# Attention values of three batches as float32 products of two heads side by side, in a fused attention and two-layer-MoE kernel

## The chip, the cores and the metric

One core of a Trainium2 chip runs the whole kernel. The metric is the device time in microseconds: before the change 1043.67 us, the median of 3 runs (1043.12 to 1044.32).

## The reference

Three stages follow each other. The change is in the last line of the first.

```python
# q, k, v: (4 batches, 8 heads, 576, 64) float32; f: (4, 8, 576)
scores = scale * q @ k^T;  cum = cumsum(log(clip(f)))
scores = where(causal, -1e9, scores + cum[..., :, None] - cum[..., None, :])
attn = exp(scores - max);  attn = attn / (sum(attn) + 1e-09)
x = attn @ v                               # then (4*576 tokens, 8*64)
x = leaky_relu(x @ w_in) @ w_out           # 512 -> 2048 -> 512
out = ((x @ w_a) * (x @ w_b)) @ w_o2       # 512 -> 1536 -> 512
```

## The kernel before

**Two kinds of product.** TensorE (PE) multiplies either operands typed float32r, of which a number is carried as a high and a low part (xh and xl, gh and gl, ph and pl), so that a product takes two or three matmuls, or plain float32 operands, where one matmul of the program makes two records of the trace. `evac` (L455 to L457) makes the two parts of a PSUM tile: ACT copies the high part, DVE subtracts it from the source for the low part. `split` does the same from SBUF (L138, L139).

**Attention in blocks.** A batch of 576 queries is done in two blocks: block 0 has the first 256 queries, block 1 the next 256 and, for two heads at once, the last 64 of each (tile p4: 64 partitions for the even head, 64 for the odd). `att_scores` makes scores, decay, maximum, exponential and the normalized probabilities of one head, with the queries on partitions. `att_values` turns (transposes) the probabilities in tiles of 128 by 128 on PE (`pp`), so that keys are on partitions, and multiplies them with v. Heads 2hp and 2hp+1 are a pair.

**The values, batch 0.** Probabilities and v are plain float32. For both heads, u = 0 and 1, the matmul's 64 value columns go to their own half of the output's partitions; the two heads' matmuls alternate, and a dependency added by hand holds the first until the second head's probabilities are there:

```python
av[u * 64 : u * 64 + 64, i0 * P : 256], vhl[:, kt, u, :], phs[u][:, a0 : a0 + 2 - i0, :],   # L533
```

**The values, batches 1 to 3.** v is split into parts side by side (`vhl`, 64 high and 64 low columns), the turned probabilities into `ph` and `pl`. Each head has its own product, two matmuls for a tile of 128 keys:

```python
for n, part in enumerate((slots, pl.rearrange("p a b c -> p (a b) c"))):
    pe_att.matmul(
        av[:, i0 * P : 256], vhl[:, kt, j, :, :], part[:, a0 : a0 + 2 - i0, :], ...   # L545 to L548
```

ACT and DVE then add the two halves of `av` (L553, L554), and after the second head the pair's 256 columns are split into the MoE's input tiles xh and xl. `att_last` turns p4 of the pair in five tiles, splits them, makes ten matmuls (`av4`, turned probabilities as weights, all four v parts moving), and ACT and DVE scale and add into x4 (L607, L608). After block 1's last pair `att_tail` turns x4 on PE (`ppx`) and splits it.

**What sets the order.** The first block is written out by hand (`FIRST`). After it the blocks are generators: the scores of one head run `beside` the values of the head before, and the last queries of a pair are chained behind its second head's values (`att_steps`). The blocks of batches 1 to 3 are interleaved with the first MoE's units (`l1` at L902 writes `h`, `l2` at L932 writes `y`; three matmuls of 256 columns a product). [...] Tiles are named buffers: `ph`, `pl`, `vs`, `vhl`, `xn` have one each, PSUM tag `ps` three.

Of the kernel before, what the change touches and what calls it, by code (L numbers as in the profile page):

```python
# [26 lines left out]
def kernel(  # L27
# [105 lines left out]
    def f32(ap):  # L133
        return ap.bitcast(F32)
# [126 lines left out]
    x4, p4s, stats, qks, xns, vhls, phs, cums, lasts, lastk = ({} for _ in range(10))  # L261
# [197 lines left out]

    def att_values(b, r, h, st):  # L460

        hp, j = h // 2, h % 2
        nk = 2 * P if r == 0 else S
        tok0 = b * S + (0 if r == 0 else 2 * P)
        nm = f"{b}_{r}_{h}"
        pair = (b, r, hp)
        ps = st["ps"]
        if j == 0:
            full, rest = nk // P, nk % P
            if b == 0:  # L470
                vs = ap_.tile([P, 5, 2, 64], F32, tag=("vs", "vhl")[hp % 2], name=f"vn_{nm}")
            else:
                vs = ap_.tile([P, 5, 2, 64], F32, tag="vs", name=f"vs_{nm}")
            for u in range(2):
                nc.sync.dma_start(vs[:, :full, u, :], v[b, h + u, : full * P, :].rearrange("(c p) d -> p c d", p=P))
                if rest:
                    nc.sync.dma_start(vs[:rest, full, u, :], v[b, h + u, full * P : nk, :])
            if b == 0:
                vhls[pair] = vs
                if rest:  # L480
                    nc.gpsimd.memset(vs[rest:, full, :, :], 0.0)
            else:

                vhl = vhls[pair] = ap_.tile([P, 5, 2, 2, 64], F32R, tag="vhl", name=f"vhl_{nm}")
                if rest:
                    nc.gpsimd.memset(f32(vhl[rest:, full, :, :, :]), 0.0)
                for x, c in ((P, slice(0, full)), (rest, slice(full, full + 1))):
                    if x:
                        split(vhl[:x, c, :, 0, :], vhl[:x, c, :, 1, :], vs[:x, c, :, :], nc.vector)
        vhl = vhls[pair]  # L490
        yield
        if b == 0:
            ph = phs[j] = ap_.tile([P, 4, 2, P], F32, tag=("ph", "pl")[j], name=f"ph_{nm}")
        else:
            ph = ap_.tile([P, 4, 2, P], F32R, tag="ph", name=f"ph_{nm}")
            pl = ap_.tile([P, 4, 2, P], F32R, tag="pl", name=f"pl_{nm}")
        slots = ph.rearrange("p a b c -> p (a b) c")
        if r == 0:

            at = {(0, 0): 1, (0, 1): 2, (1, 1): 0}  # L500
            parts = [(((1, 1), (0, 0), (0, 1)), slots[:, 0:3, :])]
        else:
            at = {(kt, i): 2 * kt + i for kt in range(4) for i in range(2)}
            parts = [([(kt, i) for kt in range(3 + i)], ph[:, : 3 + i, i, :]) for i in range(2)]
        for z, (tiles, hi) in enumerate(parts):
            pp = ps_a.tile([P, 4, P], F32, tag="ps", bufs=3, name=f"pp_{nm}_{z}")
            for m, (kt, i) in enumerate(tiles):
                pe_att.transpose(pp[:, m, :], ps[i][:, kt * P : kt * P + P], ident)
            if b == 0:
                st["second"] = act_att.copy(hi, pp[:, : len(tiles), :])  # L510
            else:
                lo = pl[:, : 3 + z, z, :] if r else pl.rearrange("p a b c -> p (a b) c")[:, 0:3, :]
                evac(hi, lo, pp[:, : len(tiles), :])
            yield
        if r == 0:
            yield
        if b == 0:
            phs[j] = slots
        if b == 0:
            if j == 0:  # L520
                return

            av = ps_a.tile([P, T1], F32, tag="ps", bufs=3, name=f"av_{nm}")
            nkt = 2 * r + 2
            for kt in range(nkt):
                i0 = 1 if kt == nkt - 1 else 0
                a0 = at[kt, i0]
                for u in range(2):
                    made = pe_att.matmul(
                        av[u * 64 : u * 64 + 64, i0 * P : 256], vhl[:, kt, u, :], phs[u][:, a0 : a0 + 2 - i0, :],  # L530
                        start=(kt == 0), stop=(kt == nkt - 1),
                    )
                    if kt == u == 0:  # L533
                        tc.add_manual_dep(made.ins, st["second"].ins.name, SYNC, reason="both heads at once")
            ch, cl = x_chunk(tok0 // T1)
            evac(ch[:, hp, :], cl[:, hp, :], av)
            yield
            return
        av = ps_a.tile([P, 256], F32, tag="ps", bufs=3, name=f"av_{nm}")
        nkt = 2 * r + 2  # L540
        for kt in range(nkt):
            i0 = 1 if kt == nkt - 1 else 0
            a0 = at[kt, i0]
            for n, part in enumerate((slots, pl.rearrange("p a b c -> p (a b) c"))):
                pe_att.matmul(  # L545
                    av[:, i0 * P : 256], vhl[:, kt, j, :, :], part[:, a0 : a0 + 2 - i0, :],
                    start=(kt == 0 and n == 0), stop=(kt == nkt - 1 and n == 1),
                )  # L548
        if j == 0:
            xns[pair] = ap_.tile([P, 256], F32, tag="xn", bufs=1, name=f"xn_{nm}")  # L550
        xt = xns[pair]
        a, o = j * 64, 64 - j * 64
        act_att.copy(xt[a : a + 64, :], av[o : o + 64, :])  # L553
        dve_att.tensor_tensor(out=xt[a : a + 64, :], in0=av[a : a + 64, :], in1=xt[a : a + 64, :], op=ALU.add)  # L554
        yield
        if j == 0:
            return
        p0 = 0
        while p0 < 256:
            c = (tok0 + p0) // T1  # L560
            c0 = tok0 + p0 - c * T1
            n = min(256 - p0, T1 - c0)
            ch, cl = x_chunk(c)
            split(ch[:, hp, c0 : c0 + n], cl[:, hp, c0 : c0 + n], xt[:, p0 : p0 + n], nc.vector)
            p0 += n
        yield

    def att_last(b, hp, rec4):
# [5 lines left out]
        ph = ap_.tile([P, 5, P], F32 if b == 0 else F32R, tag="ph", name=f"ph4_{nm}")  # L574
        nc.gpsimd.memset(f32(ph[64:, 4, :]) if b else ph[64:, 4, :], 0.0)
        if b:
            pl = ap_.tile([P, 5, P], F32R, tag="pl", name=f"pl4_{nm}")
            nc.gpsimd.memset(f32(pl[64:, 4, :]), 0.0)
        for k0, k1, w in ((0, 4, P), (4, 5, S - 4 * P)):
            pp = ps_a.tile([P, 4, P], F32, tag="ps", bufs=3, name=f"pp{k1}_{nm}")  # L580
            for kt in range(k0, k1):
                pe_att.transpose(pp[:w, kt - k0, :], p4[:, kt * P : kt * P + w], ident)
            if b == 0:
                act_att.copy(ph[:w, k0:k1, :], pp[:w, : k1 - k0, :])
            else:
                evac(ph[:w, k0:k1, :], pl[:w, k0:k1, :], pp[:w, : k1 - k0, :])
            yield
        if hp == 0:
            x4[b] = ap_.tile([P, HP // 2, P], F32, tag="x4", name=f"x4_{b}")
        if b == 0:  # L590
            av4 = ps_a.tile([P, 2, 64], F32, tag="ps", bufs=3, name=f"av4_{nm}")
            for kt in range(5):
                pe_att.matmul(av4, ph[:, kt, :], vhl[:, kt, :, :], start=(kt == 0), stop=(kt == 4))
            for u in range(2):
                rows_ = slice(u * 64, u * 64 + 64)
                act_att.mul(x4[b][64 * (hp % 2) : 64 * (hp % 2) + 64, hp // 2, rows_], av4[rows_, u, :], rec4[rows_, :])
            yield
            return
        av4 = ps_a.tile([P, 2, 2, 64], F32, tag="ps", bufs=3, name=f"av4_{nm}")
        for kt in range(5):  # L600
            pe_att.matmul(av4, ph[:, kt, :], vhl[:, kt, :, :, :], start=(kt == 0), stop=False)
            pe_att.matmul(av4, pl[:, kt, :], vhl[:, kt, :, :, :], start=False, stop=(kt == 4))
        xa = p4[:, 0:64]
        for u in range(2):
            rows_ = slice(u * 64, u * 64 + 64)
            rec = rec4[rows_, :]
            act_att.mul(xa[rows_, :], av4[rows_, u, 0, :], rec)  # L607
            dve_att.scalar_tensor_tensor(  # L608
                out=x4[b][64 * (hp % 2) : 64 * (hp % 2) + 64, hp // 2, rows_], in0=av4[rows_, u, 1, :], scalar=rec, in1=xa[rows_, :], op0=ALU.mult, op1=ALU.add
            )  # L610
# [48 lines left out]
    def first_block():  # L659
# [189 lines left out]
        def h(p, j):  # L849
            ph = ap_.tile([P, 4, 2, P], F32, tag=("ph", "pl")[j], name=f"ph_f{p}_{j}")  # L850
            x = got["ph", p, j] = ph.rearrange("p a b c -> p (a b) c")
# [410 lines left out]
    def att_steps(n):  # L1262
# [21 lines left out]
        for h in range(H):  # L1284
# [3 lines left out]
            if h % 2 == 1 and blocks[n][1] == 1:  # L1288
                second = chain(second, att_last(blocks[n][0], h // 2, st["rec4"]))
# [64 lines left out]
    for i in range(2, NB1 - 2):  # L1354
        for pr in range(NF1 // 2):
            work(i, pr)
            if pr == 0:
                for _ in att_steps(i + 1):
                    pass
                if i % 2 == 0:  # L1360
                    att_tail(i // 2)
# [139 lines left out]
```

## Time and profile before

| | |
|---|---|
| median of 3 runs | 1043.67 us (1043.12 to 1044.32) |
| the profiled execution, its span | 1049.02 us, 1047.2 us |
| PE busy, share of the span | 1017.6 us, 97% |
| PE weight loads | 942.7 us, 90% |
| DVE, ACT, POOL busy | 758.1, 586.2, 181.6 us |
| attention of batches 1 to 3 on PE | about 150 to 531 us |
| mean granted TensorE clock | 0.988 |

Matmuls are pipelined: a record of one lasts longer than the time until the next one starts. What a matmul costs PE is therefore read from the starts that follow each other, not from its length. A float32r matmul and a float32 one both carry "f32" in their shapes; the names of the operands tell them apart (float32: `vn`, `vs_f`, `kn`, `ident`; float32r: `vhl`, `ks`, `homer`). A row "x16" merges records of one kind that follow each other, at the shape of the first.

### The profile page before, as it was taken

What the parts mean: (1) busy time and instruction counts of PE and PEld (TensorE: products, weight loads), DVE (VectorE), ACT (ScalarE), POOL (GpSimd) and SP (SyncE); (2) the same over time, 40 slices, a digit from 0 to 9 for tenths busy, and PEclk for the clock granted to TensorE, in tenths of its full rate; (3) what the DMA queues carried; (4) which work ended last, traced back from release to release, by engine and by line L of the source; (5) the groups of instructions that cost most, each with busy time, mean ns of one, the idle gap of its engine ahead of it and who ended that gap; (6) DMA issues with size and microseconds to landing.
All of it is one profiled execution on the core that took longest, in us unless ns stands there. A gap on an engine that the chain in (4) does not pass through costs nothing.

```text
span 1047.2 us, 20390 instructions
## 1 busy us (share of the span) xinstructions
PE 1017.6 (97%) x7383; PEld 942.7 (90%) x7383; DVE 758.1 (72%) x1593; ACT 586.2 (56%) x1222; POOL 181.6 (17%) x414
## 2 busy tenths in 40 slices
PE   7789999999999999999999999999999999899998
PEld 6667879999999999999999998888888888799998
DVE  5869757877777777767657656787687775988872
ACT  6758777887787778868645454231323221364430
POOL 3505423334133332424100000000000000000000
PEclk9989999999999999999999999999999999999999
DMA  8788234433452334513067423222351334667721
GB/s 217 217 260 252 46 72 103 92 78 70 82 128 51 94 58 88 130 19 80 6 242 255 129 77 113 81 91 93 118 160 41 131 116 131 198 180 200 198 66 41
DMA packets 230499, 125.80 MB, mean 120 GB/s; under 512 B 144704, under 2 KB 212160, under 8 KB 230400
## 3 DMA queue, kind: packets, MB, share of 16 engines
q1 hardware_dynamic: 224784, 118.67, 41.2%
q10 hardware_dynamic: 5616, 5.84, 1.6%
q8 instruction: 58, 0.95, 0.4%
q14 instruction: 41, 0.34, 0.1%
HBM read 95.29 MB, written 29.17 MB: 119 GB/s over the span
## 4 chain that ended last, share of the span: by engine, by line
PE 81%; DMA 5%; ACT 3%; DVE 3%; issue 1%; SPq 1%; POOL 0%; ACTq 0%; DVEq 0%; POOLq 0%
PE y L932 15%; PE h L902 15%; PE o L1237 13%; PE av L99 5%; PE s L99 5%; PE b_a L1127 5%; PE b_b L1127 5%; PE pp L99 4%; PE a_a L1127 3%; PE a_b L1127 3%; PE d_b L1127 3%; PE d_a L1127 3%; PE a_last L1159 2%; PE b_last L1159 2%; DMA ty<-y_dram 1%
## 5 line engine op out<-in xcount | busy, mean ns | idle before, releaser
L902 PE MATMUL h<-xh,homer 128*128 128x256 f32 x1152 | 228.3, 284 | 2.2 <-ACT hs L915 1.5
L932 PE MATMUL y<-gh,homer 128*128 128x256 f32 x1152 | 226.0, 283 | 3.5 <-ACT gh L914 3.5
L902 PEld LDWEIGHTS h<-xh,homer 128*128 128x128 f32 x1152 | 185.6, 190 | 5.8 <-ACT hs L915 1.7
L932 PEld LDWEIGHTS y<-gh,homer 128*128 128x128 f32 x1152 | 183.2, 189 | 6.7 <-ACT gh L914 3.9
L902 PE MATMUL h<-xl,homer 128*128 128x256 f32 x576 | 163.5, 284 | 0.0
L932 PE MATMUL y<-gl,homer 128*128 128x256 f32 x576 | 161.8, 283 | 0.2 <-DVE gl L917 0.2
L932 PEld LDWEIGHTS y<-gl,homer 128*128 128x128 f32 x576 | 108.5, 188 | 1.8 <-issue 0.9
L902 PEld LDWEIGHTS h<-xl,homer 128*128 128x128 f32 x576 | 109.5, 190 | 0.3
L390 POOL TENSOR_SCALAR p<-cumb,ncum_t 128x384 f32<-128x384 f32 (+2 forms) x112 | 76.3, 689 | 144.8 <-PE pp L99 54.3
L373 ACT ACTIVATE p<-p,stat 128x256 f32<-128x256 f32 (+3 forms) x123 | 73.4, 598 | 31.5 <-DVE stat L402 22.1
L917 DVE TENSOR_TENSOR gl<-hs,gh 128x512 fp32r<-128x512 f32 x72 | 50.9, 707 | 29.9 <-ACT hs L915 29.3
L457 DVE TENSOR_TENSOR pl<-pp,ph 128x384 fp32r<-128x384 f32 (+1 forms) x96 | 53.5, 565 | 19.0 <-ACT ph L456 12.7
L411 ACT ACTIVATE p<-p,rec 128x384 f32<-128x384 f32 (+1 forms) x108 | 56.1, 568 | 13.8 <-DVE rec L379 12.9
L99 PE MATMUL pp<-ident,p 128*128 128x128 f32 (+1 forms) x376 | 60.3, 277 | 0.0
L402 DVE CUSTOM_DVE_ANT_0 p<-s,p 128x384 f32<-128x384 f32 (+2 forms) x100 | 47.6, 488 | 16.2 <-POOL p L393 9.2
L1237 PE MATMUL o<-homer,homer 128*128 128x256 f32 x441 | 57.7, 284 | 0.0
L914 ACT ACTIVATE gh<-h 128x512 fp32r<-128x512 f32 x72 | 42.5, 590 | 23.3 <-PE h L902 22.9
L1237 PEld LDWEIGHTS o<-homer,homer 128*128 128x128 f32 x441 | 55.3, 191 | 0.2
L1237 PE MATMUL o<-w_o,homer 128*128 128x256 f32 x378 | 53.2, 286 | 1.0 <-ACT homer L970 1.0
L970 ACT CAST homer<-p 128x1536 fp32r<-128x1536 f32 (+1 forms) x26 | 33.6, 1318 | 34.1 <-DVE p L995 19.7
L1237 PEld LDWEIGHTS o<-w_o,homer 128*128 128x128 f32 x378 | 49.3, 194 | 1.7 <-ACT homer L970 1.4
L456 ACT CAST ph<-pp 128x384 fp32r<-128x384 f32 (+1 forms) x96 | 45.7, 486 | 7.2 <-PE av L99 3.8
(287 smaller groups left out, 2280.1 us busy)
## 6 DMA issues: line engine op xcount, KB each, us to landing
p<-p_dram SPq DMA_DIRECT2D x17, 768.0 KB, 5.9
p_dram<-p SPq DMA_DIRECT2D x12, 1024.0 KB, 4.6
cumb<-cum_dram SPq DMA_DIRECT2D x32, 288.0 KB, 3.8
homef<-in_moe_w_out_dram SPq DMA_DIRECT2D x15, 511.6 KB, 6.0
homef<-in_moe_w_in_dram SPq DMA_DIRECT2D x15, 510.5 KB, 4.9
raw_o<-in_moe_w_out_dram SPq DMA_DIRECT2D x12, 511.6 KB, 6.1
xq<-in_q_dram SPq DMA_DIRECT2D x144, 32.0 KB, 2.0
y_dram<-yo ACTq DMA_DIRECT2D x18, 256.0 KB, 3.3
```

Source lines behind the costliest of these rows:

```text
L99: return method(*args, **kw)
L373: act_att.activation(pt, pt, AF.Exp, bias=stat[:, 0, s : s + 1], scale=-1.0, accum_out=stat[:, 1, s : s + 1])
L390: made = pool_att.tensor_scalar(pt, cumb[:, :n], 1.0, ncum_t[:, t, bh : bh + 1], op0=ALU.mult, op1=ALU.add)
L402: dve_att.tensor_tensor_reduce(out=pt, in0=sp[:, :n], in1=pt, op0=ALU.add, op1=ALU.min, scale=1.0, scalar=ABOVE, accum_out=stat[:, 0, s : ...
L411: act_att.mul(ps[i], ps[i], rec[:, i : i + 1])
L456: high = act_att.copy(hi, src)
L457: return high, dve_att.tensor_tensor(out=lo, in0=src, in1=f32(hi), op=ALU.subtract)
L902: made = nc.tensor.matmul(hps[:, u, :], w[:, c * P : c * P + P], x[:, c, :], start=(n == 0), stop=(n == 3 * ND - 1))
L917: nc.vector.tensor_tensor(out=gl, in0=hs, in1=f32(gh), op=ALU.subtract)
L932: nc.tensor.matmul(o, w[:, d * P : d * P + P], g[:, u, :], start=(fi == 0 and n == 0 and d % 2 == 0), stop=(fi == NF1 - 1 and n == 2 and d ...
L1127: nc.tensor.matmul(to, w[:, W_ROWS[m], wl, c2 * P : c2 * P + P], y[c2][xl_][:, Y_COLS[m], :], start=(first and c2 == e == 0), stop=(c2 == ...
L1237: nc.tensor.matmul(ps[m], xps[n, j // 3][:, X_ROWS[m], xl_, j % 3, :], wo2[j][:, O_COLS[m], wl, :], start=(j == e == y == 0), stop=(j == N ...
```

## The change

Batches 1 to 3 get the values as batch 0 has them: v stays float32 (no split, two buffers by turns), the turned probabilities stay float32, and the pair's two heads go to the two halves of `av`'s partitions. A new tile `pt` holds the turned probabilities of both heads by key tile; it has one buffer, and batch 0 and the first block use it in place of `ph` and `pl`. The last 64 queries of batches 1 to 3 no longer have their own product: `att_rest` normalizes p4 on ACT, turns it, and puts its columns behind each head's 256, so that block 1's product runs over 320 columns, once p4 is there. `att_tail` is left out for these batches. Batch 0 keeps `att_last` and `att_tail`.

```diff
     def att_values(b, r, h, st):
...
         if j == 0:
+            turned_p[pair] = turned_tile(nm)
             full, rest = nk // P, nk % P
+            vs = vhls[pair] = ap_.tile([P, 5, 2, 64], F32, tag=("vs", "vhl")[hp % 2], name=f"vn_{nm}")
...
-                vhl = vhls[pair] = ap_.tile([P, 5, 2, 2, 64], F32R, tag="vhl", name=f"vhl_{nm}")
...
-                        split(vhl[:x, c, :, 0, :], vhl[:x, c, :, 1, :], vs[:x, c, :, :], nc.vector)
...
-                evac(hi, lo, pp[:, : len(tiles), :])
+            if i is None:
+                act_att.copy(turned[0][:, j, 0:T1], pp[:, 0:2, :].rearrange("p m q -> p (m q)"))
+                st["second"] = act_att.copy(turned[1][:, j, P:T1], pp[:, 2, :])
             else:
+                to = turned[5][:, :2560].rearrange("p (k u q) -> p k u q", k=4, u=2)
+                st["second"] = act_att.copy(to[:, : len(tiles), j, i * P : i * P + P], pp[:, : len(tiles), :])
             yield
+        if j == 1 and (r == 0 or b == 0):
+            yield from att_product(b, r, hp, st["second"])
+
+    def att_product(b, r, hp, ready):
...
+        width = 320 if r and b else T1
+        nkt = 2 * r + 2
+        av = ps_a.tile([P, width], F32, tag="ps", bufs=3, name=f"av_{nm}")
+        for kt in range(nkt + (width > T1)):
+            q_ = (P if kt == nkt - 1 else 0) if kt < nkt else T1
+            for u in range(2):
+                made = pe_att.matmul(
+                    av[u * 64 : u * 64 + 64, q_:width], vn[:, kt, u, :], turned[kt][:, u, q_:width] if kt < 4 else turned[4][:, u, :],
+                    start=(kt == 0), stop=(kt == nkt - (width == T1)),
                 )
+                if kt == u == 0:
+                    tc.add_manual_dep(made.ins, ready.ins.name, SYNC, reason="both heads at once")
...
+            evac(ch[:, hp, c0 : c0 + n], cl[:, hp, c0 : c0 + n], av[:, p0 : p0 + n])
...
+    def att_rest(b, hp, rec4):
...
+        act_att.mul(p4, p4, rec4)
+        nc.gpsimd.memset(turned[5][64:, 2560:], 0.0)
...
+        for k0, k1, w, to in ((4, 5, S - 4 * P, tail), (0, 4, P, main)):
+            pp = ps_a.tile([P, 4, P], F32, tag="ps", bufs=3, name=f"pp{k1}_{nm}")
+            for kt in range(k0, k1):
+                pe_att.transpose(pp[:w, kt - k0, :], p4[:, kt * P : kt * P + w], ident)
+            ready = act_att.copy(to[:w], pp[:w, : k1 - k0, :].rearrange("p k (u q) -> p k u q", u=2))
+            yield
+        yield from att_product(b, 1, hp, ready)
...
             if h % 2 == 1 and blocks[n][1] == 1:
-                second = chain(second, att_last(blocks[n][0], h // 2, st["rec4"]))
+                second = chain(second, att_rest(blocks[n][0], h // 2, st["rec4"]))
...
-                if i % 2 == 0:
-                    att_tail(i // 2)
```

Two places show what moved. The first is PE in block 1 of batch 2, at the values of heads 2 and 3, before the change: the second head's product behind `h` matmuls of the MoE, then the turning of p4 (`pp_2_1_2`; the 4 of pp4 and av4 is dropped from the names).

```order
L902 MATMUL h_0_5081<-xl_3053,homer_2048_87 128x256
L99 MATMUL av_1_3_5591<-pl_1_3_5567,vhl_1_2_5452 128x256
L99 MATMUL av_1_3_5591<-ph_1_3_5566,vhl_1_2_5452 128x256
L99 MATMUL av_1_3_5591<-pl_1_3_5567,vhl_1_2_5452 128x256
L99 MATMUL av_1_3_5591<-ph_1_3_5566,vhl_1_2_5452 128x256
L99 MATMUL av_1_3_5591<-pl_1_3_5567,vhl_1_2_5452 128x256
L99 MATMUL av_1_3_5591<-ph_1_3_5566,vhl_1_2_5452 128x128
L99 MATMUL av_1_3_5591<-pl_1_3_5567,vhl_1_2_5452 128x128
L99 MATMUL pp_2_1_2_5616<-ident,p_2_1_2_5399 128x128 x4
```

The same head's matmul of `ph` on the first key tile stands 12 rows earlier, and ten `av4` matmuls follow 32 rows later. With the change the pair has one group, all its matmuls in a row; the last queries' turning stands 29 MoE matmuls and 4 score matmuls earlier:

```order
L895 MATMUL y_1_4407<-gh_6_4678,homer_2048_1357 128x256
L99 MATMUL av_1_2_5221<-pt_1_2_5084,vn_1_2_5085 64x320 x6
L99 MATMUL av_1_2_5221<-pt_1_2_5084,vn_1_2_5085 64x192 x2
L99 MATMUL av_1_2_5221<-pt_1_2_5084,vn_1_2_5085 64x64 x2
L99 MATMUL pp_1_4_0_5280<-ident,p_1_4_2_5174 128x128 x3
```

The 16 matmuls of the pair's two heads and the 10 of its last queries have become one group of 10, of half the value columns each, and the group waits for the copy of the last queries.

The second place is ACT at the same pair with the change: the copies out of the turned tiles, and the scaling of p4 (L540).

```order
L373 ACTIVATE p_2_1_2_5056,stat_1_2_4966<-p_2_1_2_5056,stat_1_2_4966 128x576
L877 ACTIVATE gh_6_4678<-h_6_4652 128x512
L878 ACTIVATE hs_6_4677<-h_6_4652 128x512
L337 ACTIVATE qhh_1_5_5253<-tq_1_5_5251 128x320
L356 CAST ks_1_6_5349<-tk_1_6_5347 64x576
L540 ACTIVATE p_2_1_2_5056<-p_2_1_2_5056,rec_1_3_4_5145 128x576
L500 COPY pt_1_2_5084<-pp_1_3_0_5183 128x3x128
L500 COPY pt_1_2_5084<-pp_1_3_1_5189 128x4x128
```

The scaling of p4 is new; the copies took the place of those at L456, and the subtractions that followed them on DVE are gone.

## Rows read from the trace of the kernel before

**Rows 1.** Busy time of each engine by stretch (length, busy us, clock, DMA).
```profile
core 0: us, PE busy (x) PEld busy (x) DVE busy (x) ACT busy (x) POOL busy (x), PEclk, DMA share, GB/s
150.00:250.00 100.00, 97.00 (x797) 95.10 (x798) 77.09 (x222) 81.79 (x210) 36.35 (x93) 1.00 0.44 91
250.00:531.00 281.00, 281.00 (x2357) 278.28 (x2356) 201.34 (x582) 211.36 (x545) 88.34 (x223) 1.00 0.33 71
531.00:600.00 69.00, 69.00 (x588) 69.00 (x587) 46.12 (x80) 35.59 (x54) 0.00 (x0) 1.00 0.66 229
```

**Rows 2.** PE's longest wait, 150 to 531 us (total us, times, longest).
```profile
PE h L902 <- ACT hs L915: 1.5, 1, 1.5
```

**Rows 3.** Instructions on tile av (count, duration ns min/median/max, first and last start).
```profile
L99 PEld LDWEIGHTS av<-ph,vhl x144: 186/188/192, 156.7 to 520.7; 128*128 128x128 f32 x144
L99 PE MATMUL av<-ph,vhl x144: 220/279/354, 156.9 to 520.8; 128*128 128x256 f32 x96, 128*128 128x128 f32 x48
...
L99 PE MATMUL av<-pl,vhl x144: 272/279/386, 157.9 to 520.9; 128*128 128x256 f32 x96, 128*128 128x128 f32 x48
L99 PEld LDWEIGHTS av<-ph,vn x64: 132/137/232, 86.4 to 144.8; 128*64 128x64 f32 x64
...
L99 PE MATMUL av<-vhl,ph x60: 277/280/284, 213.8 to 525.7; 128*128 128x256 f32 x60
...
L99 PE MATMUL av<-vhl,pl x60: 274/280/287, 213.9 to 525.8; 128*128 128x256 f32 x60
```

**Rows 4.** PE in time, batch 1: last queries' product, one head's product (start, us).
```profile
251.91 0.28 PE L99 MATMUL av<-vhl,ph 128*128 128x256 f32 x1
...
253.09 0.93 PE L99 MATMUL pp<-ident,p 128*128 128x128 f32 x7
...
259.04 0.28 PE L99 MATMUL av<-pl,vhl 128*128 128x256 f32 x1
...
259.62 0.22 PE L99 MATMUL av<-ph,vhl 128*128 128x128 f32 x1
...
259.80 0.95 PE L99 MATMUL pp<-ident,p 128*128 128x128 f32 x7
```

**Rows 5.** PE in time: the end of batch 1's last product and its tail.
```profile
271.01 0.28 PE L99 MATMUL av<-vhl,pl 128*128 128x256 f32 x1
271.22 0.34 PE L99 MATMUL ppx<-ident,x 64*128 64x64 f32 x3
271.48 0.39 PE L902 MATMUL h<-xl,homer 128*128 128x256 f32 x1
```

**Rows 6.** PE in time: batch 0's float32 products of a pair, block 0 and block 1.
```profile
27.15 0.87 PE L636 MATMUL av_f<-ph_f,vs_f 128*64 128x256 f32 x8
27.95 0.44 PE L636 MATMUL pp_f<-ident,p_f 128*128 128x128 f32 x2
...
86.23 0.28 PE L902 MATMUL h<-xh,homer 128*128 128x256 f32 x1
86.44 1.73 PE L99 MATMUL av<-ph,vn 128*64 128x256 f32 x16
88.10 0.77 PE L99 MATMUL pp<-ident,p 128*128 128x128 f32 x5
```

**Rows 7.** Busy time and clock, 141.8 to 145.3 us (columns as in rows 1).
```profile
141.80:145.30 3.50, 3.50 (x19) 1.80 (x17) 3.16 (x13) 2.13 (x8) 0.06 (x1) 0.51 0.47 72
```

**Rows 8.** PE in time around that stretch (start, us).
```profile
139.97 0.65 PE L99 MATMUL pp<-ident,p 128*128 128x128 f32 x4
...
142.14 3.24 PE L99 MATMUL av<-ph,vn 128*64 128x256 f32 x16
145.31 0.77 PE L99 MATMUL pp<-ident,p 128*128 128x128 f32 x5
```

**Rows 9.** ACT by group, 150 to 531 us (count, busy us, mean ns, idle before).
```profile
L373 ACT ACTIVATE p<-p,stat 128x576 f32<-128x576 f32 x12 | 9.3, 778 | 5.9 <-DVE stat L444 5.8
```

**Rows 10.** DVE by group, 150 to 531 us.
```profile
L457 DVE TENSOR_TENSOR pl<-pp,ph 128x384 fp32r<-128x384 f32 x48 | 26.3, 549 | 7.2 <-PE s L99 2.9 <-ACT ph L456 1.7 <-POOL p L393 1.5
```

More of the change, by code (lines that the diff above doesn't have):

```diff
@@ L259, in x_chunk @@
         return xh[c], xl[c]
-    x4, p4s, stats, qks, xns, vhls, phs, cums, lasts, lastk = ({} for _ in range(10))
+    x4, p4s, stats, qks, turned_p, vhls, phs, lasts, lastk = ({} for _ in range(9))
     def att_scores(b, r, h, st):
@@ L457, in evac, with turned_tile @@
         return high, dve_att.tensor_tensor(out=lo, in0=src, in1=f32(hi), op=ALU.subtract)
+    def turned_tile(name):
+        t = ap_.tile([P, 2688], F32, tag="pt", name=f"pt_{name}")
+        return [t[:, 640 * kt : 640 * kt + 640].rearrange("p (u q) -> p u q", u=2) for kt in range(4)] + [
+            t[:, 2560:].rearrange("p (u q) -> p u q", u=2),
+            t,
+        ]
     def att_values(b, r, h, st):
@@ L468, in att_values @@
         if j == 0:
+            turned_p[pair] = turned_tile(nm)
             full, rest = nk // P, nk % P
[L470 to L473, printed above, removed]
+            vs = vhls[pair] = ap_.tile([P, 5, 2, 64], F32, tag=("vs", "vhl")[hp % 2], name=f"vn_{nm}")
             for u in range(2):
@@ L477, in att_values @@
                     nc.sync.dma_start(vs[:rest, full, u, :], v[b, h + u, full * P : nk, :])
[L478 to L481, printed above, removed]
-            else:
-                vhl = vhls[pair] = ap_.tile([P, 5, 2, 2, 64], F32R, tag="vhl", name=f"vhl_{nm}")
[L485 to L488, printed above, removed]
-                        split(vhl[:x, c, :, 0, :], vhl[:x, c, :, 1, :], vs[:x, c, :, :], nc.vector)
@@ L490, in att_values @@
[L490 to L512, printed above, removed]
-                evac(hi, lo, pp[:, : len(tiles), :])
+            if rest:
+                nc.gpsimd.memset(vs[rest:, full, :, :], 0.0)
@@ new lines, in att_values @@
+        turned = turned_p[pair]
+        yield
+        parts = [([(kt, 0) for kt in range(2 * r + 1)], 0), ([(kt, 1) for kt in range(2 * r + 2)], 1)]
+        if r == 0:
+            parts = [([(0, 0), (0, 1), (1, 1)], None)]
+        for z, (tiles, i) in enumerate(parts):
+            pp = ps_a.tile([P, 4, P], F32, tag="ps", bufs=3, name=f"pp_{nm}_{z}")
+            for m, (kt, i_) in enumerate(tiles):
+                pe_att.transpose(pp[:, m, :], ps[i_][:, kt * P : kt * P + P], ident)
+            if i is None:
+                act_att.copy(turned[0][:, j, 0:T1], pp[:, 0:2, :].rearrange("p m q -> p (m q)"))
+                st["second"] = act_att.copy(turned[1][:, j, P:T1], pp[:, 2, :])
+            else:
+                to = turned[5][:, :2560].rearrange("p (k u q) -> p k u q", k=4, u=2)
+                st["second"] = act_att.copy(to[:, : len(tiles), j, i * P : i * P + P], pp[:, : len(tiles), :])
@@ L516, in att_values @@
             yield
[L517 to L538, printed above, removed]
@@ L539, in att_values @@
-        av = ps_a.tile([P, 256], F32, tag="ps", bufs=3, name=f"av_{nm}")
-        nkt = 2 * r + 2
[L541 to L547, printed above, removed]
-                )
@@ L549, in att_values @@
[L549 to L557, printed above, removed]
+        if j == 1 and (r == 0 or b == 0):
+            yield from att_product(b, r, hp, st["second"])
+    def att_product(b, r, hp, ready):
+        pair = (b, r, hp)
+        nm = f"{b}_{r}_{2 * hp}"
+        turned, vn = turned_p[pair], vhls[pair]
+        tok0 = b * S + 2 * P * r
+        width = 320 if r and b else T1
+        nkt = 2 * r + 2
+        av = ps_a.tile([P, width], F32, tag="ps", bufs=3, name=f"av_{nm}")
[5 more added lines that the diff above has]
+                    start=(kt == 0), stop=(kt == nkt - (width == T1)),
+                )
+                if kt == u == 0:
+                    tc.add_manual_dep(made.ins, ready.ins.name, SYNC, reason="both heads at once")
@@ L558, in att_values @@
         p0 = 0
-        while p0 < 256:
+        while p0 < width:
             c = (tok0 + p0) // T1
             c0 = tok0 + p0 - c * T1
-            n = min(256 - p0, T1 - c0)
+            n = min(width - p0, T1 - c0)
             ch, cl = x_chunk(c)
-            split(ch[:, hp, c0 : c0 + n], cl[:, hp, c0 : c0 + n], xt[:, p0 : p0 + n], nc.vector)
+            evac(ch[:, hp, c0 : c0 + n], cl[:, hp, c0 : c0 + n], av[:, p0 : p0 + n])
             p0 += n
         yield
+    def att_rest(b, hp, rec4):
+        pair = (b, 1, hp)
+        nm = f"{b}_1_{2 * hp}"
+        turned, p4 = turned_p[pair], p4s[b, hp]
+        act_att.mul(p4, p4, rec4)
+        nc.gpsimd.memset(turned[5][64:, 2560:], 0.0)
+        main = turned[5][:, :2560].rearrange("p (k u q) -> p k u q", k=4, u=2)[:, :, :, T1:320]
+        tail = turned[5][:, 2560:].rearrange("p (k u q) -> p k u q", k=1, u=2)
+        for k0, k1, w, to in ((4, 5, S - 4 * P, tail), (0, 4, P, main)):
[3 more added lines that the diff above has]
+            ready = act_att.copy(to[:w], pp[:w, : k1 - k0, :].rearrange("p k (u q) -> p k u q", u=2))
+            yield
+        yield from att_product(b, 1, hp, ready)
@@ L573, in att_last @@
         p4 = p4s[b, hp]
[L574 to L578, printed above, removed]
+        ph = turned_tile(f"4_{nm}")[5][:, :640].rearrange("p (k q) -> p k q", k=5)
+        nc.gpsimd.memset(ph[64:, 4, :], 0.0)
         for k0, k1, w in ((0, 4, P), (4, 5, S - 4 * P)):
@@ L582, in att_last @@
                 pe_att.transpose(pp[:w, kt - k0, :], p4[:, kt * P : kt * P + w], ident)
[L583 to L586, printed above, removed]
+            act_att.copy(ph[:w, k0:k1, :], pp[:w, : k1 - k0, :])
             yield
@@ L589, in att_last @@
             x4[b] = ap_.tile([P, HP // 2, P], F32, tag="x4", name=f"x4_{b}")
[L590 to L599, printed above, removed]
+        av4 = ps_a.tile([P, 2, 64], F32, tag="ps", bufs=3, name=f"av4_{nm}")
         for kt in range(5):
-            pe_att.matmul(av4, ph[:, kt, :], vhl[:, kt, :, :, :], start=(kt == 0), stop=False)
-            pe_att.matmul(av4, pl[:, kt, :], vhl[:, kt, :, :, :], start=False, stop=(kt == 4))
-        xa = p4[:, 0:64]
+            pe_att.matmul(av4, ph[:, kt, :], vhl[:, kt, :, :], start=(kt == 0), stop=(kt == 4))
         for u in range(2):
             rows_ = slice(u * 64, u * 64 + 64)
[L606 to L610, printed above, removed]
+            act_att.mul(x4[b][64 * (hp % 2) : 64 * (hp % 2) + 64, hp // 2, rows_], av4[rows_, u, :], rec4[rows_, :])
         yield
@@ L849, in h @@
         def h(p, j):
-            ph = ap_.tile([P, 4, 2, P], F32, tag=("ph", "pl")[j], name=f"ph_f{p}_{j}")
-            x = got["ph", p, j] = ph.rearrange("p a b c -> p (a b) c")
+            pt = tile_of(("pt", p), lambda: turned_tile(f"f{p}")[5])
+            x = got["ph", p, j] = pt[:, 640 * j : 640 * j + 384].rearrange("p (m q) -> p m q", q=P)
             got["last", p] = act.copy(x[:, 0:3, :], got["pp", p, j][:, 0:3, :])
```

## The prediction

> **What bounds the kernel now.** I read the busy times by stretch first. From 150 to 531 us, where the values of batches 1 to 3 are made between the first MoE's units, PE is idle for 3.0 us of the first 100 and for none of the next 281, at the full clock; DVE is busy 72 to 77% and ACT 75 to 82% of the time [rows 1]. The reader is to see two things there: PE sets the pace of the whole stage, and it goes on doing so after attention has ended, 531 to 600 us, with 69.00 of 69.00 busy [rows 1]. So a slot taken away on PE is time off the end, and what leaves ACT and DVE counts only where PE waits for them, which is little: the longest wait is 1.5 us, for an `hs` of ACT [rows 2]. Then I read the instructions on `av`, for the counts, and PE in order of time, for the slots.
>
> **What is taken off PE.** Rows 3 hold 144 + 144 matmuls of the heads' products and 60 + 60 of the last queries'. Block 0's heads (24) have 4 each, block 1's (24) have 8, the 12 pairs' last queries 10. Their slots, from start to start:
> - a 256-column matmul: from 259.04 to 259.62 five of them, 0.117 us each; the last two, of 128 columns, 259.62 to 259.80, 0.18 together [rows 4];
> - a head of block 1: 0.117 + (259.80 - 259.04) = 0.88, and 24 x 0.88 = 21.1 us;
> - a head of block 0: 2 x 0.117 + 0.18 = 0.41, and 24 x 0.41 = 9.8 us;
> - last queries: 253.09 - 251.91 = 1.18, and 12 x 1.18 = 14.2 us [rows 4];
> - tails: three of the four `ppx` run from 271.13 (start of the last `av` plus 0.117) to 271.48, 0.35 [rows 5]; the fourth stands alone, and I give it 0.25 as a switch in and out; three batches, 1.8 us.
>
> Sum 46.9 us.
>
> **What is put on PE.** Batch 0's float32 groups are the same instructions, 64 value columns for each half. A group of block 0 takes 27.95 - 27.15 = 0.80 us, one of block 1 takes 88.10 - 86.44 = 1.66 us [rows 6]. In columns for one half, with two records a matmul, the first is 2 x (256 + 128) = 768 and the second 2 x (3 x 256 + 128) = 1792. The slope is 0.86 / 1024 = 0.84 ns a column, the rest 0.155 us a group. The way in costs 0.21 instead of 0.12 (86.23 to 86.44), 0.09 more.
> - Block 0: 0.80 + 0.09 = 0.89, 12 pairs, 10.7 us. That is a little more than the 0.82 of the two heads that it replaces: by itself this half of the change loses 0.8 us.
> - Block 1: 2 x (3 x 320 + 192 + 64) = 2432 columns, 0.155 + 2.04 + 0.09 = 2.29 us. Upper bound: the narrow 64-column records cost as much as 128-column ones, 0.11 more, 2.40. Lower bound: the slope alone, 2.04 + 0.09 = 2.13. I take 2.3, since the fixed rest shows in both rows; 12 pairs, 27.6 us, with 25.6 and 28.8 as ends.
>
> Sum 38.3 us; the turnings of probabilities and of p4 (`pp`) stay in number. The balance is 46.9 - 38.3 = 8.6 us off PE, nearly all of it from the last queries, whose ten matmuls and tails (16.0 us) become 64 more columns in a group that runs anyway.
>
> **What the other engines get and lose.** DVE loses the low parts of the turned tiles (48 of 549 ns for 384 columns, 26.3 us, and as much again for the wider and narrower ones [rows 10]), and the additions on `av`, the splits of v and the scaling of x4. ACT loses the splits and halves likewise, and gains 12 scalings of p4; the exponential of the same 128 x 576 takes 778 ns [rows 9], so 9.3 us, and 24 extra small copies. This lies beside PE's work, and costs nothing as long as PE has MoE matmuls to go on with: between the last queries' turning and the group that needs them stand 29 of these, 3.4 us, against a copy or two on ACT. On SP the loads of v are the same in number, and with two buffers they wait for the pair before last instead of the last one; POOL's zeroing of the tiles no longer waits for the product of the pair before. If the cover went, `av`, the first in PE's queue, would hold up all that stands behind it (a rival below). For the lighter ACT and DVE I credit a third of PE's 3.0 idle us, 1.0; its ends are 0 and 3.0.
>
> The forecast is 8.6 + 1.0 = 9.6 us less: 1039.4 for an execution like the profiled one (1049.02), which stands 5.35 above the median; against the median, 1043.67 - 9.6 = **1034.1 us**.
>
> **A rule weighed here.** PE's weight loads are busy for 278.28 of 281 us [rows 1], and a load takes 188 ns for 128 columns and 137 for 64 [rows 3]. If the loads set the slots, 408 of 188 ns (76.7 us, in 45.1 us of slots) would make way for 336 of 137 (46.0 us, in 27.1 at the same ratio), and the gain with the tails would be 19.8 us, 1023.9. Against it: batch 0's group packs 16 loads of 137 ns into 1.66 us, 0.104 each, and its slots follow the columns that are streamed [rows 6]. I sum by columns. [...]
>
> **The rivals.**
> - *Weight loads set the slots*: 1024, as above; chance 0.03. With it goes a stage whose order also profits from lighter engines, 1027 or so if all 3.0 us and the lower bounds come: 0.04.
> - *The group waits* (this one ends on the slower side). Now every head's product starts when its own parts are there; with the change 24 groups stand in PE's queue, in order, until the second head's copy or the p4 copy has landed. `pt` has one buffer, so the next pair's copies wait in turn for the group. For it: p4's path has one more step of about 0.78 us on ACT. Against it: the 29 matmuls ahead, and lighter ACT and DVE. It decides from 9.6 / 24 = 0.40 us a group; at 0.2 the time is 1039, at 0.6 it is 1048.5. Chance 0.13, of which 0.04 ends slower.
> [...]
> - *The halves do not run side by side* for 320 columns, so that the change does not do what it says: the group's columns count twice, 12 x (2.04 + 0.65) = 32 us more, 1066. Batch 0's rows speak against it: 1.66 us is what one half needs. Chance 0.02.
>
> **How the numbers follow.** The forecast, a gain of 5 to 14 us, has 0.72; the two kinds of a larger gain 0.07; the waiting group 0.13; the clock 0.05; the halves 0.02; 0.01 is left for the rest. A measurement of this kernel tells 0.2%, 2.1 us, from no change. Slower by over that: 0.04 of the waits, 0.02 of the clock and 0.02 of the halves, 0.08 in all. Within it: 0.06, from the waits and the clock. Faster: 0.86. The range: the ends of the priced terms give 1034.1 - 4.0 = 1030 (2.0 on block 1, 2.0 on the idle time) and 1034.1 + 2.2 (1.2 and 1.0) = 1036; the waits up to 0.27 us a group reach to 1040.5, and I stop there.
>
> **What would show it.** In the profile after: groups of 20 records on `av<-vn,pt` or its like, about 2.2 us from first to next, and of 8 records, 0.80; PE idle under 3 us in the stage; attention's last group near 515 us; DVE's busy time in the stage down by about a third, with no effect of its own on the span. Starts of a group at half clock, PE waits put down to the `pt` copies, or groups of over 2.5 us at full clock would show me wrong.

## The result, and the profile after

The changed kernel takes 1033.6 us, the median of 4 runs (1030.66 to 1034.15), against 1043.99 (1043.12 to 1047.0) before: ratio 0.989, 95% interval 0.9862 to 0.9917. The forecast was 1034.1. Beside the experiments the changed kernel ran three times more, with ratios of 0.9875 (0.9848 to 0.9902), 0.9902 (0.9878 to 0.9927) and 0.9885 (0.9849 to 0.992): by the medians it is 10.4 to 12.3 us faster. Two executions fell into a much slower state, one of experiment 8 (1641.65 us) and one of the kernel before beside experiments 10 and 11 (1415.03 us), and are left out of all medians and ratios.

The profiled execution took 1030.66 us, with a span of 1028.9: 18.3 us under the profile of before. That is more than the change brings: the one is the quickest of its four runs, the other (1049.02) slower than all of its four. So the two traces are compared by stage, from a mark that both have: the start of batch 0's last float32 group (142.14 us before [rows 8]) to the first matmul of the second MoE, which PE reaches in the trace of before at

```profile
639.34 0.98 PE L1127 MATMUL a_a<-ys,w_a 128*128 128x512 f32 x3 [1.18 <-ACT yo L940]
```

and in the trace of after, in time on PE, at

```profile
135.72 3.25 PE L99 MATMUL av<-pt,vn 128*64 128x256 f32 x16
...
620.60 0.96 PE L1090 MATMUL a_a<-ys,w_a 128*128 128x512 f32 x3 [1.18 <-ACT yo L903]
```

497.2 us before, 484.9 after: the stage gained 12.3. Behind it nothing changed (1047.2 - 639.3 = 407.9, 1028.9 - 620.6 = 408.3), so 6.4 us of the 18.3 came ahead of the mark; the first experiment shows how much they vary from run to run.

A second mark, further on and free of the slow group at the stage's start, is the first MoE matmul behind batch 0's attention: the 385th record of `h` and `y`, at 146.38 us before and 140.03 after. The busy times from there to the first matmul of the second MoE, before and after (columns as in rows 1: length, PE, weight loads, DVE, ACT, POOL, clock, DMA):

```profile
146.38:639.34 492.96, 488.56 (x4089) 483.26 (x4087) 352.17 (x934) 352.42 (x850) 124.69 (x316) 1.00 0.39 98
```

```profile
140.03:620.60 480.57, 477.89 (x4004) 456.97 (x4003) 264.93 (x724) 323.77 (x772) 122.09 (x304) 1.00 0.41 101
```

The stage lost 12.4 us by this mark too. PE is still the bound: it is idle for 2.7 of 480.6 us after, for 4.4 of 493.0 before. So 10.7 of the 12.4 us are work that left PE, and 1.7 are idle time. From 250 us to the end of attention PE is never idle:

```profile
250.00:500.00 250.00, 250.00 (x2087) 236.93 (x2086) 125.03 (x385) 174.60 (x440) 80.72 (x198) 1.00 0.35 74
```

Its waits in the stage, 147 to 615 us, are two:

```profile
PE h L865 <- ACT hs L878: 0.9, 1, 0.9
PE s L99 <- DVE stat L402: 0.6, 1, 0.6
```

No group waits for the copies into `pt`. The instructions on `av` now are one kind of record and batch 0's own products (count, duration ns, first and last start), where there were 408 of float32r [rows 3]; and two groups in time, one of block 1 and one of block 0:

```profile
L99 PE MATMUL av<-pt,vn x400: 219/379/687, 80.1 to 499.4; 128*64 128x320 f32 x48, 128*64 128x256 f32 x31, 128*64 128x128 f32 x23, 128*64 128x192 f32 x16
L99 PE MATMUL av<-vn,pt x40: 271/275/275, 86.7 to 143.0; 128*128 128x128 f32 x40
```

```profile
210.71 2.27 PE L99 MATMUL av<-pt,vn 128*64 128x320 f32 x20
212.92 0.98 PE L99 MATMUL pp<-ident,p 128*128 128x128 f32 x7
...
256.54 0.28 PE L865 MATMUL h<-xl,homer 128*128 128x256 f32 x1
256.75 0.87 PE L99 MATMUL av<-pt,vn 128*64 128x256 f32 x8
257.55 0.50 PE L865 MATMUL h<-xh,homer 128*128 128x256 f32 x2
```

A group of 20 records takes 2.21 us, one of 8 takes 0.80, and the way in 0.21 instead of 0.12, as rows 6 had it for batch 0.

### The profile page after: what moved, and what is told of

Same layout as the page of the kernel before. It is cut to its first block, busy times and chain, and to the rows that moved or that the text cites. A ratio compares the mean times of both kernels' runs of the same rounds, so it can differ in the third digit from the quotient of the medians.

```text
span 1028.9 us, 19822 instructions
## 1 busy us (share of the span) xinstructions
PE 1005.5 (98%) x7299; PEld 913.8 (89%) x7299; DVE 671.6 (65%) x1383; ACT 557.9 (54%) x1144; POOL 178.4 (17%) x402
## 4 chain that ended last, share of the span: by engine, by line
PE 92%; DMA 4%; ACT 1%; DVE 1%; POOL 1%; issue 1%; SPq 0%; ACTq 0%; POOLq 0%; DVEq 0%
PE h L865 19%; PE y L895 19%; PE o L1200 12%; PE s L99 6%; PE b_b L1090 5%; PE b_a L1090 5%; PE av L99 5%; PE pp L99 4%; PE a_a L1090 3%; PE a_b L1090 3%; PE d_b L1090 3%; PE d_a L1090 3%; DMA homef<-in_moe_w_out_dram 2%; PE a_last L1122 2%; PE b_last L1122 2%; DMA homef<-o_dram 1%
## 5 line engine op out<-in xcount | busy, mean ns | idle before, releaser
L865 PE MATMUL h<-xh,homer 128*128 128x256 f32 x1152 | 225.6, 283 | 0.9 <-ACT hs L878 0.9
L865 PEld LDWEIGHTS h<-xh,homer 128*128 128x128 f32 x1152 | 183.4, 188 | 5.6 <-issue 2.7
L99 PEld LDWEIGHTS pp<-ident,p 128*128 128x128 f32 (+1 forms) x376 | 43.4, 139 | 4.0 <-issue 2.3
L99 PE MATMUL av<-pt,vn 128*64 128x320 f32 (+4 forms) x400 | 46.9, 372 | 0.0
```

Of the source, the lines that this page charges most:

```text
L99: return method(*args, **kw)
L865: made = nc.tensor.matmul(hps[:, u, :], w[:, c * P : c * P + P], x[:, c, :], start=(n == 0), stop=(n == 3 * ND - 1))
```

## The experiments

**1. The changed kernel again.** No edit.

> The changed kernel once more, as the mark for the others and to see how much of its profile belongs to chance. Between the profiles of before and after, the time up to the end of batch 0's MoE work (the 384th matmul of h and y) differs by 6.3 us (146.4 against 140.0), the stage from there to the first matmul of the second MoE by 12.4 us (493.0 against 480.6), the rest by nothing. Slots theory (PE sets the pace, and the gain is the slots that left PE): the stage is again 480 to 482 us, the time 1031 to 1035. Relief theory (the gain comes from lighter ACT and DVE, which also reach the first stage): the first stage ends near 140 us again, every time.

1032.57 us, ratio 0.9875. From the second mark (the 385th matmul of `h` and `y`) the stage was 482.7 us long, and 480.1 and 480.3 in the two later repeats (runs 7 and 9), where the first profile after had 480.6 and the one before 493.0. The first stage is another matter: that 385th matmul began at 137.0 us here, at 145.8 and 143.1 in the repeats of the same program, at 140.0 in the first profile. Two repeats over 62 to 90 us, busy time and clock, the quick one (this run) and the slow one (run 7):

```profile
62.00:90.00 28.00, 26.06 (x175) 19.65 (x176) 27.20 (x54) 25.69 (x48) 14.20 (x16) 1.00 0.88 251
```

```profile
62.00:90.00 28.00, 23.69 (x125) 17.89 (x124) 20.03 (x41) 20.61 (x37) 5.44 (x9) 0.76 0.76 218
```

In the slow one PE waits once for 3.33 us, for an ACT step, and the granted clock is 0.76 in the mean of the stretch, where the quick one has 1.00:

```profile
66.14 0.79 PE L895 MATMUL y<-gh,homer 128*128 128x256 f32 x2 [3.33 <-ACT gh L877]
```

The profile of before has the same picture, a wait of 3.13 us and a clock of 0.88 from 62 to 90 us:

```profile
68.89 0.80 PE L932 MATMUL y<-gh,homer 128*128 128x256 f32 x2 [3.13 <-ACT gh L914]
```

So the 6.4 us ahead of the mark lie within what one program shows from run to run (8.8 us between the quickest and the slowest of its four profiles), and the medians, 10.4 to 12.3 us apart, leave no room for them beside the stage. That the change has no part in them at all isn't shown. A single profile against another tells nothing under 9 us of this kernel; the stage, 480.1 to 482.7 us in four profiles, tells 3.

**2. The last queries apart.** The streaming of the last queries is taken out: the pair's product stays float32, at 256 columns, and the last 64 queries get batch 0's treatment.

```diff
-        width = 320 if r and b else T1
+        width = T1
-        if j == 1 and (r == 0 or b == 0):
+        if j == 1:
-                second = chain(second, att_rest(blocks[n][0], h // 2, st["rec4"]))
+                second = chain(second, att_last(blocks[n][0], h // 2, st["rec4"]))
+                if i % 2 == 0:
+                    att_tail(i // 2)
```

> The pair's float32 product stays, at 256 columns in block 1 too; the last 64 queries get their own float32 product and the turning of x4 back, as batch 0 has them. Slots theory: a group of block 1 costs 1.66 + 0.09 = 1.75 us against 1.76 for the two heads before, the last queries ten records of 0.11, 1.1 to 1.2 us against 1.18, block 0 loses 0.8 in all, so the gain is gone but for what idle time the lighter engines save: 1041.5 to 1044.5. Relief theory: DVE and ACT stay as light as in the changed kernel (no low parts, no splits of v), so most of the gain stays: 1033 to 1037.

1044.45 us, ratio 1.0003 (0.9977 to 1.0029): the whole gain is gone, with the two lighter engines kept. Busy times from 150 to 500 us in this run, DVE 187.0 and ACT 254.1 us (186.2 and 255.2 in the changed kernel, under experiment 5):

```profile
150.00:500.00 350.00, 348.87 (x2906) 331.43 (x2906) 187.01 (x587) 254.08 (x669) 123.29 (x303) 1.00 0.40 83
```

Its PE in time shows why the gain is gone, one pair's last queries and another pair's group:

```profile
200.89 1.27 PE L99 MATMUL av<-vn,pt 128*128 128x128 f32 x10
202.00 0.49 PE L99 MATMUL pp<-ident,p 128*128 128x128 f32 x3
...
228.60 1.74 PE L99 MATMUL av<-pt,vn 128*64 128x256 f32 x16
230.27 0.76 PE L99 MATMUL pp<-ident,p 128*128 128x128 f32 x5
```

The group takes 1.67 us (and 0.09 for the way in) where two heads took 1.76, the last queries 1.11 where they took 1.18: float32 on halves costs PE what the float32r parts cost. The gain is in what the last queries no longer need. The profiled execution was the slowest of its twelve (1053.25 us), with PE waits of 3.4 us in the MoE behind attention, so its stage isn't compared.

**3. Block 0 alone.** In the kernel before, block 0 of batches 1 to 3 takes batch 0's branch.

```diff
+        flat = b == 0 or r == 0
...
-        if b == 0:
+        if flat:
```

(at each place in `att_values`; the pair's columns are then split by input tile, as the change does.)

> The kernel before, with block 0 of batches 1 to 3 alone made as float32 products of two heads; block 1 and the last queries as before. Slots theory: 12 groups of 0.89 us for 12 times 0.82, so 0.8 us slower, within what can be measured: 1043.5 to 1045.5. Relief theory: DVE loses 24 subtractions of 0.55 us, 24 additions of 0.42 and the splits of v, some 29 us, a third of its relief: 2 to 4 us faster, 1040 to 1042.

1047.2 us, ratio 1.002 (0.9999 to 1.004): no faster, rather a little slower. From the second mark on, its stage:

```profile
142.17:638.01 495.84, 489.25 (x4089) 478.21 (x4087) 328.16 (x878) 338.25 (x814) 125.71 (x316) 1.00 0.40 98
```

PE's busy time is 0.7 us above the kernel before (488.56), as the slots have it (0.8). The other 2.2 us of this stage are idle time, 6.6 for 4.4 us, in one profile; whether they come with the edit isn't shown. DVE got lighter by 24 us, and the time shows nothing of it.

**4. One head after the other.** The two loops of a product exchanged.

```diff
-        for kt in range(nkt + (width > T1)):
-            q_ = (P if kt == nkt - 1 else 0) if kt < nkt else T1
-            for u in range(2):
+        for u in range(2):
+            for kt in range(nkt + (width > T1)):
+                q_ = (P if kt == nkt - 1 else 0) if kt < nkt else T1
```

> The changed kernel with the two loops of a product exchanged: all matmuls of the first head, then all of the second, instead of one of each by turns. Same matmuls, same columns. Slots theory with the halves side by side only where they alternate: a group of block 1 needs 2.04 us more, one of block 0 0.65, with 12 of each 32 us, and batch 0's four groups of 1.51 add 6: 1069 to 1073. If the halves would overlap in whatever order they stand, or if they never did: 1033 to 1035.

1056.41 us, ratio 1.0109 (1.0068 to 1.015): about 24 us slower than the changed kernel beside it (1032.57), which neither expectation had. Its groups of block 1 and block 0:

```profile
214.93 3.94 PE L99 MATMUL av<-pt,vn 128*64 128x320 f32 x20
218.80 0.98 PE L99 MATMUL pp<-ident,p 128*128 128x128 f32 x7
...
265.97 0.88 PE L99 MATMUL av<-pt,vn 128*64 128x256 f32 x8
266.77 0.50 PE L865 MATMUL h<-xh,homer 128*128 128x256 f32 x2
```

A group of block 1 lost 1.66 us (3.87 for 2.21), not 2.04; a group of block 0 lost nothing (0.80), though its second head stands behind four records of the first. 12 x 1.66, and 0.9 for each of batch 0's four groups of block 1, are 23.5 of the 24 us. By the starts of single records, the second head's first (320 columns) starts 6 ns behind the first head's seventh of ten (192 columns), and in block 0 some 13 ns behind its first of four. Experiments 10 and 11 take that up.

**5. DVE's subtractions put back.** Behind each copy of turned probabilities of batches 1 to 3:

```diff
+            if b:
+                n = 2 * P if i is None else len(tiles) * P
+                old = ps[1 if i is None else i][:, :n]
+                dve_att.tensor_tensor(out=old, in0=pp.rearrange("p a q -> p (a q)")[:, :n], in1=old, op=ALU.subtract)
```

> The changed kernel, with the subtractions on DVE put back for batches 1 to 3: behind each copy of turned probabilities, DVE subtracts from the same PSUM tile the same number of columns (256 in block 0, 384 and 512 in block 1), into the probabilities' own tile, which is not read after that. Results stay the same. Some 40 us of work in the stage return to DVE, of the about 100 that it lost. Slots theory: PE hardly waits, so 0 to 1 us slower, 1033 to 1035. Relief theory: 40% of the gain goes back, 4 us or more, 1037.5 or later.

1034.43 us, ratio 0.9908 (0.989 to 0.9927), beside 0.9902 of the changed kernel in the same group. From 150 to 500 us, this run:

```profile
150.00:500.00 350.00, 348.93 (x2904) 329.41 (x2905) 218.91 (x644) 253.15 (x646) 119.02 (x296) 1.00 0.38 80
```

and the changed kernel's first profile:

```profile
150.00:500.00 350.00, 349.37 (x2909) 329.28 (x2908) 186.16 (x580) 255.16 (x650) 118.75 (x296) 1.00 0.39 81
```

33 us went back to DVE (not 40); PE's busy time and the result did not move.

**6. Batch 0 too.** Its last queries are streamed along; their columns wait in x4 for their input tile.

```diff
-        width = 320 if r and b else T1
+        width = 320 if r else T1
+            if b == 0 and p0 == T1:
+                if hp == 0:
+                    x4[b] = ap_.tile([P, HP, 64], F32, tag="x4", name=f"x4_{b}")
+                act_att.copy(x4[b][:, hp, :], av[:, T1:width])
+                break
-                    before = chain(before, att_last(0, h // 2, sts[h + 1]["rec4"]))
+                    before = chain(before, att_rest(0, h // 2, sts[h + 1]["rec4"]))
```

> The changed kernel with batch 0 treated alike: its last 64 queries are streamed with the other 256 of block 1, their columns are kept in the x4 tile and split into their input tile at the same place as before; its own ten matmuls per pair and the turning of x4 are gone. Slots theory: four times 1.09 us and about 0.2 of switches against 64 more columns (0.54 us), and one tail of 0.6: 3 to 3.6 us off PE, less what PE idles there anyway (28.3 of 30 us busy from 120 to 150): 1030 to 1032. Relief theory, or if the start of the kernel is not bound by PE: no change against the changed kernel, 1033 to 1034.

1034.81 us, ratio 0.9901 (0.9881 to 0.9921), for 0.9902 without it: nothing gained, a miss of the slots theory. PE in time at the batch's last pair:

```profile
137.95 0.45 PE L99 MATMUL s<-ks,qhh 128*128 128x128 f32 x1 [1.18 <-ACT qhh L337]
...
143.49 4.32 PE L99 MATMUL av<-pt,vn 128*64 128x320 f32 x20 [1.19 <-ACT pt L553]
147.74 1.00 PE L99 MATMUL pp<-ident,p 128*128 128x128 f32 x6
```

```profile
127.50:148.50 21.00, 17.33 (x91) 10.49 (x90) 12.23 (x46) 14.95 (x41) 5.23 (x14) 0.76 0.32 64
136.50:147.50 11.00, 8.12 (x35) 5.07 (x34) 7.07 (x27) 7.54 (x23) 0.58 (x2) 0.56 0.39 69
```

Here the rival of the waiting group is seen at last: no MoE matmuls stand ahead, the group waits 1.19 us for the copy of the last queries, and the granted clock is 0.56 from 136.5 to 147.5 us; the group takes 4.25 us, where one took 2.21 at a clock of 1.00. An early group of this run, from 110.72 us, ran as fast as in the other batches (2.20). But the order changed as well: PE has no MoE matmul from 127.5 to 148.5 us, 21 us with 91 records of attention, where four profiles of the changed kernel have 8.6 to 10.2 us with about 52. PE idles for 3.7 us of that (0.8 in those), and the last group alone takes 2.0 us more than at a clock of 1.00 (4.25 for 2.21): in this run, the slowest of its six, more than the 3 to 3.6 us that were to be saved. How much of it stands in the median, which moved by less than the first stage varies (experiment 1), isn't shown.

**7. The changed kernel again**, the mark of experiments 5 and 6.

> The changed kernel, beside the two runs of this group as their mark. Both theories: 1031 to 1035, the same ratio to the kernel before as in the other group within 0.3%.

1033.39 us, ratio 0.9902 (0.9878 to 0.9927).

**8. Block 1 alone**, the counterpart of 3: in the changed kernel, block 0 of batches 1 to 3 goes back to `att_values` of before.

```diff
-            second = att_values(*blocks[n], h, st)
+            second = (att_values if blocks[n][1] else att_values_first)(*blocks[n], h, st)
```

> The other half of the change: block 1 and the last queries of batches 1 to 3 as in the changed kernel, block 0 with float32r parts and one product a head, as before. Slots theory: 12 times 0.82 us in place of 12 times 0.89, so 0.8 us faster than the changed kernel, if the splits and low parts that return to ACT and DVE cost PE nothing: 1032 to 1034 where the changed kernel has about 1033. Relief theory: a third of the relief goes back, 1034 to 1037. If block 0 alone really costs the 0.2% that the third experiment leans to, 1031 to 1032.

1031.43 us, ratio 0.9879 (0.9841 to 0.9917). Its stage from the second mark on:

```profile
140.90:620.12 479.22, 476.59 (x4004) 461.22 (x4003) 292.92 (x788) 334.36 (x784) 118.93 (x304) 1.00 0.41 101
```

PE is busy for 476.6 us, 1.3 less than in the changed kernel, with DVE 28 and ACT 11 us heavier. **9. The changed kernel beside it**

> The changed kernel as the mark beside it: 1031 to 1035, as in the other two groups.

took 1032.09 us, ratio 0.9885 (0.9849 to 0.992). Block 1 with the last queries is worth all of the gain; block 0 is worth nothing that the medians tell, and costs PE about 1 us.

**10 and 11. Turns of two and of three key tiles.** The loop of experiment 4, cut.

```diff
-        for kt in range(nkt + (width > T1)):
...
-            for u in range(2):
+        nk_ = nkt + (width > T1)
+        for u, kt in [(u, kt) for k0 in range(0, nk_, 2) for u in range(2) for kt in range(k0, min(k0 + 2, nk_))]:
```

(with 3 in place of 2 in the other.)

> The changed kernel with two key tiles of the first head, then two of the second, by turns (four records each). In the fourth experiment, all of one head ahead of the other, a group of block 0 (4 records a head) still took 0.81 us, while in groups of 8 and 10 records a head the second head's first record started beside the first head's fifth and seventh: each time with three records of the first head passed over. If PE passes over up to three records whose half is taken, turns of four records cost nothing: groups of 2.2 us, 1031 to 1035. If the overlap in block 0 had another reason (its length, its shapes), groups of block 1 lose at each turn, 0.3 us or more a group: 1037 or later.

> The same with three key tiles a turn (six records). If up to three records are passed over, the second head starts beside the third record of the first, two records late: about 0.54 us more in each of the 12 groups of block 1, 0.43 in the 4 of batch 0, 8 us in all: 1039 to 1043, groups of 2.75 us. If any number could be passed over: 1031 to 1035. If none: at each turn a whole stretch runs alone, 1050 or later.

Turns of two: 1033.62 us, ratio 0.9904 (0.9879 to 0.9929). Turns of three: 1039.84, ratio 0.9967 (0.9936 to 0.9997). A group of block 1, first with turns of two, then of three:

```profile
209.30 2.33 PE L99 MATMUL av<-pt,vn 128*64 128x320 f32 x20
211.56 0.98 PE L99 MATMUL pp<-ident,p 128*128 128x128 f32 x7
```

```profile
213.99 2.86 PE L99 MATMUL av<-pt,vn 128*64 128x320 f32 x20
216.79 0.98 PE L99 MATMUL pp<-ident,p 128*128 128x128 f32 x7
```

2.26 and 2.80 us, for 2.2 and 2.75 expected: within 0.06 us of what was worked out for a PE that passes over up to three records whose half is taken, and no more.

## Why the prediction was right

**The bound.** PE set the pace before and after. In the stage DVE lost 87 us and ACT 29 (352.2 to 264.9, 352.4 to 323.8), and that bought no more than the idle time below: with 33 us of DVE's back (experiment 5) the gain stayed, and with all of the relief but without the streamed queries (experiment 2) it was gone.

**The slots put on.** 2.21 + 0.09 for a group of block 1 (2.29 worked out from the slope, 2.3 taken) and 0.80 + 0.09 for one of block 0. The narrow records followed the slope (0.055 us for 64 columns in experiment 4, 0.86 ns a column); the upper bound for them was not needed.

**The slots taken off.** The forecast's split, block 0 worth -0.8 us and all the rest in the last queries, is what the experiments show: block 0 cost PE 0.7 us (3) and 1.3 (8), and without the streamed last queries nothing was left (2).

**Where the sum was too small.** 8.6 us of slots and 1.0 of idle time were forecast; the stage shows 10.7 and 1.7. PE's time in the stage, counted in the two traces from each record's start to the next one's, with waits of over 0.05 us taken off:

| records | before, us | after, us | change | forecast |
|---|---|---|---|---|
| heads' products, groups (`av`) | 32.0 | 36.2 | +4.1 | +5.2 |
| last queries (`av4`) and tails (`ppx`), batch 0's among them | 17.4 | 1.7 | -15.8 | -16.0 |
| turnings (`pp`) | 26.5 | 25.1 | -1.4 | 0 |
| scores (`s`) | 44.5 | 43.4 | -1.1 | 0 |
| MoE (`h`, `y`) | 368.0 | 371.5 | +3.5 | +2.2, the ways in |

The terms that were priced came out within 1.3 us each. Turnings and scores, whose number stayed and which were put at no change, gave 2.5 us; the order of the records around them changed, and no run shows which neighbour makes them cheaper. In all, two repeats (7 and 9) have 478.1 us and the third (1) 479.6, for 477.9 in the first profile. The idle time fell by 1.3 to 2.4 us in the four profiles, more than the 1.0 credited and inside its ends of 0 and 3.0. That the median came within 0.5 us of the forecast is in part luck: the gain, 10.4 us in that comparison and 10.5 to 12.3 in the three others, was above the 9.6 forecast each time.

**A sign that did not come.** Attention's last group was to start near 515 us; it started at 497.3, and at 495.0 to 502.6 in the repeats. 6.4 us of that are the quick first stage, and 84 more MoE matmuls stand behind the group than before (1025 for 941), some 10 us of work that only changed its place.

**The weighed rule.** Weight loads are busy for 236.93 of 250 us after, where they were busy for 278.28 of 281 [rows 1]: their share fell by 4 points and PE stayed as full as before. Had the loads set the slots, the stage would have gained 19.8 us; it gained 12.3. The busy share of the loads, 99 and 95%, doesn't price the change; the starts that follow each other do.

**The rivals.** The group didn't wait in batches 1 to 3, where 20 to 30 MoE matmuls stand between the turning of p4 and each of the 12 groups, and did in batch 0 (experiment 6), where there are none: PE stood idle for 1.19 us ahead of it. The clock, which has 0.05 of the forecast's chances, was 1.00 in the stage from the second mark on (its row), also where group, turning and scores stand behind each other, from 210.71 to 216 us, and 1.00 from 150 to 500 us in runs 1, 2, 5, 6 and 7: a fall in batches 1 to 3 is in none of these. Even the low clock at the end of batch 0 [rows 7] comes and goes with the run: the group there took 3.18 us in the first profile after, at a clock of 0.50, and 1.67 in three repeats of the same program (run 7 has a clock of 1.00 from 136.5 to 147.5 us, around its group). The halves ran side by side at 320 columns; experiment 4 shows the price when they don't, 1.66 us a group.

## What to carry to other kernels

Where PE is full, count slots from start to start in the trace, part by part: here the half of the edit that looked like the change, plain float32 on halves in place of split operands, cost PE about 1 us and brought nothing, and the 64 columns that rode along in a group that ran anyway were worth 1%. Relief on engines that PE doesn't wait for was worth what its idle rows say (1.7 us), not what the relief measures (87 us of DVE). And compare single profiles by stages that both share: the first stage of one program differed by up to 8.8 us from run to run, with an early wait of 3.33 us and a clock of 0.76 around it in the slowest.

## What the runs showed of the hardware

In these float32 groups the matmuls on the two halves of the output's partitions need not alternate in the program. Turns of four records cost 0.05 us a group (2.26 for 2.21), turns of six 0.59, ten in a row 1.66; that is as if PE started a later record while up to three ahead of it wait for the other half. The starts are not those of the program's order either: in experiment 4 the records of a group of block 0 start in pairs some 13 ns apart and end after 0.80 us, where the program has four of one head, then four of the other.

In experiment 4 a float32 matmul of these groups costs two records, each of 0.269 us from start to start at 320 columns, 0.162 at 192 and 0.055 at 64 (one half alone): 0.84 to 0.86 ns a column.
